# Loads by pairs of head groups, one solve load per chunk, five stores issued by ScalarE, and a refitted planner in a chunked RWKV and two-layer MLP kernel

## The chip, the cores and the metric

The kernel runs on one core of one Trainium2 chip. The metric is the device time of one execution in microseconds. Three runs of the kernel before gave 1331.51 us as their median (1323.21 to 1335.31).

## The reference

The first part is a recurrence over 768 steps for 4 batches x 8 heads with head size 40. Its output, laid out as 3072 tokens x 320, goes through two MLPs with 2048 hidden units.

```python
for t in range(S):
    y[:, :, t] = np.einsum('bhd,bhde->bhe', rt, state)
    Sa = np.einsum('bhde,bhe->bhd', state, at)
    state_decay = state * wt[:, :, None, :] - np.einsum('bhd,bhe->bhde', Sa, bt)
    state = state_decay + np.einsum('bhd,bhe->bhde', vt, kt)
...
h = np.maximum(x @ w_in, 0.0); x = h * h @ w_out
...
h = x @ w_in; g = np.where(h > 0.0, h, np.exp(np.minimum(h, 0.0)) - 1.0); out = g @ w_out
```

## The kernel before

The sequence is cut into 12 chunks of 64 steps. The 32 pairs of batch and head are worked on in 4 units of 8 (`hs(u)`). Within a chunk the recurrence becomes matrix products, and only the state is passed on from chunk to chunk. The MLPs work on the 256 tokens of a chunk.

For each chunk c, the steps that matter here are these, by function name.

- `scan`, `prep_a`, `prep_r`, `kb_rows`: running products of the decay, a and r scaled and split into three bf16 parts; the results go to the scratch tensors p_scr, a_scr, ya_scr and r_scr in device memory.
- `gram(c, u)` (line 954): loads ag from a_scr and gy from ya_scr (three loads, by `load_stacks`, line 883), multiplies gx with gy into PSUM (gram), masks one half into ag with VectorE, and copies the other half into bs with ScalarE. SP then stores bs to b_scr. bs has one buffer, so the copy of the next unit needs the store before it to have landed.
- `block_load(c, u)` (991) loads the 16 x 16 diagonal blocks of unit u from b_scr into the tile w, which the trace calls tt (free in chunk 1). `block_rest` (995) loads the other parts into lz (pb) and tb. `block_step` (1004) is the triangular solve: 15 steps of two VectorE instructions on w, which need all four units. `block_store` (1011) sends the result through n_scr and t_scr and loads it back as n1 (nt) and tb. `block_join` joins the blocks with small matmuls (join).
- `load_dyn(c, u)` (1065) loads vu, rf, rq (three loads by `load_stacks`) and w0 of one unit. The `dyn_*` functions are the part that depends on the state: f, u, bu, s (the new state), gh (which reads rq) and y. y goes to x_scr in device memory.
- `mlp1(c)` (782) loads x from x_scr, rounds it into xhi and xlo (`split_x`, 664) and runs the first MLP: h in PSUM (two buffers), its eviction by ScalarE, then accA and accB. `mlp2(c)` runs the second MLP.

The weights of both MLPs are loaded and converted in 24 pieces each (cs, ct; wl is TensorE's part of it). In two early chunks some tiles of odd units lie in weight tiles that are not yet filled (free); their PSUM tiles are called early.

The order of the instructions isn't the order of the code. The class `Order` records every operation of the main part, gives it a key (a due time from the tables OFF, SHIFT and BIAS plus 16 per chunk), and plays a list schedule: each engine takes, of the operations that are ready, the one with the lowest score. The costs in `cost` and constants such as ISSUE and SLOW say how long the planner takes an operation to be; `run` keeps a model of the clock and of the DMA rings. `emit` (522) writes the operations in the planned order, each engine's queue in that order, so all these instructions have one line in the profile (L527). Each engine executes its queue strictly in that order, SP's DMA issues too.

```python
AG, GX, BS, RAW, PL, VU, RV, W0, GH = 7, 1, 1, 2, 1, 2, 2, 2, 1
...
i = getattr(getattr(self.nc, name), op)(*a, **k)
```

Of the kernel before, what the change touches and what calls it, by code (L numbers as in the profile page):

```python
# [11 lines left out]
F32 = mybir.dt.float32  # L12
# [12 lines left out]
C = 64  # L25
NC = S // C
U = 4
HU = NH // U
# [21 lines left out]
T_W2, T_CL = 171, 197.1  # L50
OFF = {
# [9 lines left out]
}  # L61
SHIFT = {
    "prep": [-154.4, -2.921, -6.123, -4.768, -1.157, -0.04128, -7.933, -4.66, -8.011, -6.105, -9.653, -10.29],
    "gram": [-112.7, -7.051, -7.963, -1.157, -4.153, -5.312, -11.74, -10.6, -7.853, -6.692, -7.601, -13],
    "solve": [-21.31, -3.896, -6.557, 1.652, 0.3282, -6.306, -2.684, 6.628, 2.2, -4.088, -3.429, -14.15],
    "dyn": [-0.7973, -1.841, -2.488, 4.568, 0.9962, -2.788, -5.72, 5.713, 1.11, -2.128, -3.253, -3.913],
    "mlp": [-8.911, -10.83, -8.953, -8.113, -4.064, -4.485, -6.448, -8.254, -8.7, 3.455, 28.13, 32.75],
    "w": [-0.5978, -82.63, -108.8, -425.3, 353, 9.79, -83.32, 559.7, 134.3, 158.3, 376.1, -44.56],
    "mlp2": [24.41, 162.4, 191.8, 295.3, 373.5, 419.9, 490.2, 518.4, 570.3, 669.1, 674.1, 675.8],
}  # L70
BIAS = {
    "scan": [13.45, 2.846, 10.1, 3.45, -1.11, -3.105, 1.682, 21.9, 0, -2.434, 0.791, -0.6537],
# [125 lines left out]
class Order:  # L198
# [41 lines left out]
    def add(self, name, op, a, k):  # L240
# [13 lines left out]
        for aps, write in ((ins, False), (outs, True)):  # L254
            for x in aps:
# [10 lines left out]
                for e in h:  # L266
                    p, w, l2, h2 = e
                    hit = all(x1 <= y2 and x2 <= y1 for x1, y1, x2, y2 in zip(lo, hi, l2, h2))
                    if hit and (write or w) and p is not o:
                        o.deps.add(p)  # L270
# [1183 lines left out]
```

## Time and profile before

| what | value |
|---|---|
| median of three runs | 1331.51 us |
| the profiled execution | 1333.78 us |
| its span (first to last instruction) | 1331.9 us |
| mean granted TensorE clock | 0.925 |
| TensorE matmul busy (PE) | 1216.2 us, 91% |
| TensorE weight load busy (PEld) | 1113.1 us, 84% |
| VectorE busy (DVE) | 765.2 us, 57% |
| ScalarE busy (ACT) | 797.3 us, 60% |
| GpSimd busy (POOL) | 505.8 us, 38% |
| DMA | 158.01 MB, 119 GB/s in the mean |

The profile is of one execution on one core. A row of the timeline gives the start in us from the span's start, the duration, the engine, the operation with its output and inputs, and in brackets the idle time just before it with what ended it. A granted clock of 1.00 is full speed. SPq is SP's queue, which issues DMAs; the duration of such a row is that of the issue, not of the transfer. All names are the program's tile names without their buffer numbers.

### The profile page before, as it was taken

To read this page: it belongs to the slowest core of one execution; us is meant where nothing else is said; L and a number is where in the kernel's file an instruction comes from. 1 tells how busy PE (TensorE), PEld (TensorE's weight loads), DVE (VectorE), ACT (ScalarE), POOL (GpSimd) and SP (SyncE) were. 2 spreads that over 40 slices of the span, in tenths; PEclk is the share of its full clock that TensorE was granted. 3 is DMA by queue.
4 is the path that set the end of the run, shared out by engine and by line. 5 is a ranking of instruction groups with operands and counts; after the bars stand their busy time and mean duration, and the time that the engine had idled before them with its cause. 6 is when DMAs were issued, how large, how long until landed. Compare 5 with 4: busy or idle time off the path is not lost. (4 is left out here: it accounts for less than half of the span.)

```text
span 1331.9 us, 41778 instructions
## 1 busy us (share of the span) xinstructions
PE 1216.2 (91%) x17409; PEld 1113.1 (84%) x17409; DVE 765.2 (57%) x1434; ACT 797.3 (60%) x1536; POOL 505.8 (38%) x485
## 2 busy tenths in 40 slices
PE   2567879999999999999999999999999999999996
PEld 1446658789888988889888999999999999999996
DVE  6487766836743758666557634568844434434432
ACT  4576476647454657375576345555666666666663
POOL 2252131334441355243343222467733333333332
PEclk8667678979986999899999999999999999999998
DMA  8887885666565585655565423343300000000000
GB/s 269 227 226 173 225 214 149 168 158 166 135 171 128 156 211 142 164 119 151 133 179 146 93 61 108 101 142 115 94 21 21 21 21 21 21 21 21 21 16 17
DMA packets 244947, 158.01 MB, mean 119 GB/s; under 512 B 165648, under 2 KB 214160, under 8 KB 244752
## 3 DMA queue, kind: packets, MB, share of 16 engines
q1 hardware_dynamic: 244752, 155.27, 44.3%
q8 instruction: 139, 2.28, 0.7%
q14 instruction: 56, 0.46, 0.1%
HBM read 114.52 MB, written 40.69 MB: 117 GB/s over the span
## 5 line engine op out<-in xcount | busy, mean ns | idle before, releaser
L527 PE MATMUL h<-xhi,w 128*128 128x256 f32 x1920 | 513.6, 298 | 6.7 <-DVE r L527 6.0
L527 POOL TENSOR_TENSOR glo<-r,ghi 128x512 fp32r<-128x512 f32 x192 | 255.7, 1334 | 446.4 <-ACT ghi L527 208.6
L527 PEld LDWEIGHTS h<-xhi,w 128*128 128x128 f32 x1920 | 358.7, 192 | 24.6 <-DVE r L527 14.9
L527 PE MATMUL h<-xlo,w 128*128 128x256 f32 x1152 | 325.2, 285 | 0.0
L527 PEld LDWEIGHTS h<-xlo,w 128*128 128x128 f32 x1152 | 221.3, 192 | 0.3 <-POOL xlo L527 0.2
L527 ACT ACTIVATE r<-h 128x512 f32<-128x512 f32 x192 | 114.5, 596 | 134.7 <-PE h L527 123.1
L527 DVE SCALAR_TENSOR_TENSOR r<-e,r 128x512 f32<-128x512 f32 x96 | 75.6, 787 | 197.5 <-ACT r L527 197.4
L527 DVE TENSOR_TENSOR r<-h,r 128x512 f32<-128x512 f32 x192 | 132.2, 689 | 88.9 <-ACT ghi L527 76.8
L527 PE MATMUL accA<-w,ghi 128*128 128x320 f32 x768 | 179.4, 315 | 2.4 <-ACT ghi L527 2.3
L527 PE MATMUL accB<-w,ghi 128*128 128x320 f32 x768 | 178.4, 314 | 0.4 <-DVE o L527 0.4
L527 PEld LDWEIGHTS accA<-w,ghi 128*128 128x128 f32 x768 | 125.1, 191 | 4.2 <-ACT ghi L527 3.3
L527 PEld LDWEIGHTS accB<-w,ghi 128*128 128x128 f32 x768 | 125.4, 191 | 1.3 <-DVE o L527 0.6
L527 PE MATMUL accA<-w,glo 128*128 128x320 f32 x384 | 123.4, 321 | 1.3 <-POOL glo L527 0.7
L527 PE MATMUL accB<-w,glo 128*128 128x320 f32 x384 | 123.8, 322 | 0.0
L527 ACT CAST ghi<-r 128x512 fp32r<-128x512 f32 x96 | 59.1, 616 | 46.9 <-PE accB L527 23.5
L527 DVE SCALAR_TENSOR_TENSOR tt<-tt 128x1 f32<-128x1 f32 (+4 forms) x165 | 72.9, 442 | 24.6 <-DMA tt<-b_scr 20.0
L527 ACT ACTIVATE ghi<-r 128x512 fp32r<-128x512 f32 x96 | 60.4, 631 | 32.3 <-PE accB L527 31.4
L527 PEld LDWEIGHTS accA<-w,glo 128*128 128x128 f32 x384 | 73.3, 191 | 2.9 <-POOL glo L527 1.4
L527 PEld LDWEIGHTS accB<-w,glo 128*128 128x128 f32 x384 | 73.4, 191 | 1.4
L527 POOL TENSOR_TENSOR raw<-raw,pl 128x640 f32<-128x640 f32 x23 | 34.0, 1477 | 83.9 <-ACT pl L527 45.5
L527 PEld LDWEIGHTS <-gx 120*128 120x128 bf16 x1152 | 44.9, 108 | 25.0 <-issue 14.4
L527 POOL TENSOR_TENSOR kd<-kbt,ks 128x320 f32<-128x320 f32 x42 | 36.4, 866 | 77.1 <-ACT ks L527 77.1
(157 smaller groups left out, 2201.3 us busy)
## 6 DMA issues: line engine op xcount, KB each, us to landing
gy<-ya_scr SPq DMA_DIRECT2D x144, 120.0 KB
rq<-r_scr SPq DMA_DIRECT2D x144, 120.0 KB
cs<-w SPq DMA_DIRECT2D x32, 512.0 KB
kbt<-kbt SPq DMA_DIRECT2D x12, 640.0 KB
cs<-w SPq DMA_DIRECT2D x16, 384.0 KB
b_scr<-bs SPq DMA_DIRECT2D x48, 128.0 KB
ya_scr<-pl SPq DMA_DIRECT2D x12, 480.0 KB
r_scr<-pl SPq DMA_DIRECT2D x12, 480.0 KB
```

Of the source, the lines that this page charges most:

```text
L527: i = getattr(getattr(self.nc, name), op)(*a, **k)
```

## The change

Five edits, and one that follows from them.

- rq is one tile for a pair of units (`pair(u)`, 16 heads), filled by three loads when the even unit is loaded. There is one such buffer (RV // 2) where there were two single ones.
- ag is one tile for a pair, its lower part filled by one load. There are three such buffers where there were seven single ones.
- The diagonal blocks of all four units come in one load of 128 partitions (`block_load(c)`, due at what was the fourth unit's place) instead of four of 32.
- The four stores of bs to b_scr and the store to n_scr are issued by ScalarE (`nc.scalar.dma_start`), the rest of the DMAs by SP as before.
- The planner charges a DMA to the engine that issues it, takes 350 where it took 410 for an issue (plus 110 where one follows close on another on SP), has other constants for the clock, and orders VectorE and ScalarE where both touch one PSUM tile.
- All due times and biases are new numbers.

The matmuls, the operations of VectorE, ScalarE and GpSimd and their shapes are the same in number; SP has 192 DMA issues fewer and ScalarE 60 more.

```diff
-T_W2, T_CL = 171, 197.1
+T_W2, T_CL = 176.1, 213.4
-SWITCH, THIN, CHILL, BUSY = 0.1452, 5.835, 749.1, 0.5074
-YIELD = {"PE": (977.1, 24.8, 40.11), "DVE": (0.1731, 13.95, 2.022e+09), "ACT": (0.3328, 0.739, 1.114e+06), "POOL": (0.129, 32.88, 2.894e+05), "SP": (17.1, 0.6629, 215)}
-HOLD = {"PE": (2.65, 686.8), "DVE": (0.02736, 2.751e+04), "ACT": (0.2812, 674), "POOL": (1.353, 1.238), "SP": (0, 7.007)}
-ISSUE, STORE, LOAD, GUARD, COOL, WARM = 410.0, 2100.0, 2100.0, 600.0, 0.37, 0.6
-SLOW = {"b_scr": 300.0, "t_scr": 310.0, "tb": 160.0, "cs": 80.0, "vu": 200.0, "vs": 150.0, "wx": 80.0, "raw": 100.0, "n_scr": 250.0, "out": 100.0, "nt": 150.0, "rf": 50.0, "x": 100.0, "tt": 50.0, "k_scr": 100.0}
+SWITCH, THIN, CHILL, BUSY = 0.09435, 7.919, 28.43, 0.6976
+YIELD = {"PE": (2.587e+06, 6.959, 80.92), "DVE": (0.1309, 2.937, 5.164e+09), "ACT": (0.2351, 0.03413, 686.2), "POOL": (0.0002282, 4.888, 2.397e+06), "SP": (136.9, 4.725, 220)}
+HOLD = {"PE": (1.841, 924.1), "DVE": (0.7854, 9.898e+05), "ACT": (0.01352, 234.3), "POOL": (1.027e-05, 29.14), "SP": (0, 0.01961)}
+CLOSE = 110.0
+ISSUE, STORE, LOAD, GUARD, COOL, WARM = 350.0, 2100.0, 2100.0, 600.0, 0.40, 0.77
+SLOW = {"b_scr": 300.0, "t_scr": 310.0, "tb": 150.0, "cs": 60.0, "vu": 170.0, "vs": 170.0, "wx": 90.0, "raw": 90.0, "n_scr": 150.0, "out": 160.0, "nt": 100.0, "x": 40.0, "k_scr": 90.0, "a_scr": 80.0, "p_scr": 80.0}
...
-    "scan": -27.24, "pa": -24.91, "pr": -9.754, "kb": -27.22, "pl0": -19.04, "gr0": -17.12, "bl0": -9.569, "pl1": -19.19, "gr1": -17.24, "bl1": -13.25, "pl2": -18.08, "gr2": -14.83,
+    "scan": -27.03, "pa": -24.12, "pr": -14.35, "kb": -26.05, "pl0": -21.09, "gr0": -19, "pl1": -19.93, "gr1": -18.75, "pl2": -16.7, "gr2": -16.04, "pl3": -16.37, "gr3": -12.38,
...
-        self.clock, self.window, self.area, self.mode = 1.0, 0.0, 0.0, None
+        self.clock, self.window, self.area, self.mode = 0.5, 0.0, 0.0, None
-        self.tail = {"DVE": 0.0, "ACT": 0.0}
+        self.tail = {"DVE": 0.0, "ACT": 0.0, "SP": 0.0}
...
-                    if hit and (write or w) and p is not o:
+                    if (hit and (write or w) or t.space == PSUM and o.eng != p.eng and "PE" not in (o.eng, p.eng)) and p is not o:
...
-        if name == "sync":
+        if op == "dma_start":
...
-            o.area += stream * rep / 2.4 * min(1, rows / 128) * min(1, cols / 128)
+            o.area += stream * rep / 2.4 * max(r, 64) * max(c, 64) / 16384
...
-        if p.eng == "SP":
+        if p.dma is not None:
...
-            o.wait = o.eng in self.tail and any(p.eng != o.eng for p in o.deps)
+            o.wait = o.eng in ("DVE", "ACT") and any(p.eng != o.eng for p in o.deps)
...
-            o.late = max(o.late, p.end + (HOLD["SP"][1] if p.eng == "SP" else 0.0))
+            o.late = max(o.late, p.end + (HOLD["SP"][1] if p.dma is not None else 0.0))
...
-        elif o.eng == "SP":
-            self.free["SP"] = at + d
+        elif o.dma is not None:
+            if o.eng == "SP" and at - self.tail["SP"] < 150:
+                d += CLOSE
+            self.free[o.eng] = self.tail[o.eng] = at + d
...
-            if o.eng in self.tail:
+            if o.eng != "POOL":
...
 
+        def pair(u):
+            return slice(u * HU, (u + 2) * HU)
+
         def halves(u):
...
 
-        def load_stacks(dst, scr, u):
-            src = scr[:, hs(u)].rearrange("e n q t -> e (n q t)")
+        def load_stacks(dst, scr, heads):
+            src = scr[:, heads].rearrange("e n q t -> e (n q t)")
             for q in range(3):
...
         def gram(c, u):
-            ag = p1.tile([104, HU, C], F32, tag="ag", bufs=AG, name="ag")
+            if u % 2 == 0:
+                ex[c, u // 2, "ags"] = p1.tile([104, 2 * HU, C], F32, tag="ag", bufs=AG // 2, name="ag")
+                nc.sync.dma_start(out=ex[c, u // 2, "ags"][64:104], in_=a_scr[c][:, pair(u)])
+            ag = ex[c, u // 2, "ags"][:, hs(u % 2)]
             ex[c, u, "ag"] = ag
-            nc.sync.dma_start(out=ag[64:104], in_=a_scr[c][:, hs(u)])
             early = c < EP and u % 2
             gy = (mlp if early else p0).tile([120, HU, 3, C], BF16, tag="xhi" if early else "gy", bufs=XB if early else GX, name="gy")
-            load_stacks(gy, ya_scr[c], u)
+            load_stacks(gy, ya_scr[c], hs(u))
             gx = (mlp if early else p0).tile([120, HU, 2 * C], BF16, tag="r" if early else "gx", bufs=2 if early else GX, name="gx")
...
             nc.scalar.copy(out=flat(bs)[b], in_=flat(ps)[b])
-            nc.sync.dma_start(out=ap(b_scr[c][:], u * HU * HB, [[C, C], [HB, HU], [1, C]]), in_=bs[b])
+            nc.scalar.dma_start(out=ap(b_scr[c][:], u * HU * HB, [[C, C], [HB, HU], [1, C]]), in_=bs[b])
 
...
 
-        def block_load(c, u):
-            nc.sync.dma_start(
-                out=ex[c, "w"][32 * u:32 * u + 32, 0], in_=ap(b_scr[c][:], u * HU * HB, [[HB // 4, 32], [C, 16], [1, 16]]))
+        def block_load(c):
+            nc.sync.dma_start(out=ex[c, "w"][:, 0], in_=ap(b_scr[c][:], 0, [[HB // 4, 128], [C, 16], [1, 16]]))
 
...
             nc.scalar.copy(out=w[:, 0], in_=w[:, 1].rearrange("p r t -> p t r"))
-            nc.sync.dma_start(out=n_scr[c].rearrange("n h t r -> (n h) t r"), in_=w[::2, 0])
+            nc.scalar.dma_start(out=n_scr[c].rearrange("n h t r -> (n h) t r"), in_=w[::2, 0])
             for q in range(2):
...
             nc.sync.dma_start(out=rf, in_=io["rt"][c][:, hs(u)])
-            rq = p1.tile([120, HU, 3, C], BF16, tag="rq", bufs=RV, name="rq")
-            ex[c, u, "rq"] = rq
-            load_stacks(rq, r_scr[c], u)
+            if u % 2 == 0:
+                ex[c, u // 2, "rqs"] = p1.tile([120, 2 * HU, 3, C], BF16, tag="rq", bufs=RV // 2, name="rq")
+                load_stacks(ex[c, u // 2, "rqs"], r_scr[c], pair(u))
+            ex[c, u, "rq"] = ex[c, u // 2, "rqs"][:, hs(u % 2)]
             w0 = p1.tile([D, HU, C + 1], F32, tag="w0", bufs=W0, name="w0")
...
                 at("gram", f"gr{u}", c, lambda u=u: gram(c, u))
-                at("gram", f"bl{u}", c, lambda u=u: block_load(c, u))
+            at("gram", "bl3", c, lambda: block_load(c))
 
         def solve(c):
             at("gram", "bn", c, lambda: blocks(c))

```

SP's queue around the solve of chunk 0, before: b_scr_111 is chunk 0's scratch, ag and a_scr_76 belong to chunk 1, cs are weight pieces.

```order
L527 DMA b_scr_111<-bs 64x8x64
L527 DMA tb<-b_scr_111 32x8x32
L527 DMA ag<-a_scr_76 40x512 x4
L527 DMA tt<-b_scr_111 32x16x16
L527 DMA tb<-b_scr_111 32x8x32
L527 DMA b_scr_111<-bs 64x8x64
L527 DMA ya_scr_88<-pl 128x5x384
L527 DMA raw<-ax 128x640
L527 DMA cs<-w 128x1024 x2
L527 DMA tt<-b_scr_111 32x16x16
L527 DMA pb<-b_scr_111 16x32x16 x2
```

The same place on SP after the change.

```order
L528 DMA tb<-b_scr_111 32x8x32
L528 DMA ag<-a_scr_76 40x1024 x2
L528 DMA tb<-b_scr_111 32x8x32
L528 DMA cs<-w 128x768
L528 DMA ya_scr_88<-pl 128x5x384
L528 DMA tt<-b_scr_111 128x16x16
L528 DMA pb<-b_scr_111 16x32x16 x2
```

The stores are gone from SP, the loads tt are one, and one weight piece of 384 KB stands ahead of it where two of 512 KB stood.

ScalarE's queue from the third copy of bs to the fourth, chunk 0, before.

```order
L527 COPY bs<-gram 64x512
L527 ACTIVATE cs<-cs 128x512
L527 CAST pl<-raw 128x10x64
L527 ACTIVATE cs<-cs 128x384
L527 CAST w_182<-cs 128x512
L527 COPY bs<-gram 64x512
```

And after the change.

```order
L528 COPY bs<-gram 64x512
L528 DMA b_scr_111<-bs 64x8x64
L528 CAST pl<-raw 128x10x64
L528 COPY bs<-gram 64x512
L528 DMA b_scr_111<-bs 64x8x64
L528 CAST w_179<-wl 128x2x64
```

Each copy is followed by its own store, and the weight conversions stand behind the last of them.

TensorE's queue at the first matmul of the MLP (h), before. nt and pb are chunk 2's, y, gh and kbt chunk 1's.

```order
L527 MATMUL fa<-vs,ag 64x40 x16
L527 MATMUL str<-ident,vs 40x40 x8
L527 MATMUL y<-gh,kbt 40x64 x8
L527 MATMUL join<-nt,pb 32x16 x32
L527 MATMUL h<-xhi,w_178 128x256
L527 MATMUL h<-xlo,w_178 128x256
```

And after the change, where the y from rf is unit 0 of chunk 1, the first y that reads the state.

```order
L528 MATMUL wl<-cs,ident 128x128
L528 MATMUL wl<-w_446,minus 128x128
L528 MATMUL h<-xhi,w_178 128x256
L528 MATMUL h<-xlo,w_178 128x256
L528 MATMUL y<-rf,ss_193 40x64 x8
L528 MATMUL y<-gh,kbt 40x64 x8
```

The first h has moved ahead of that y and so ahead of the rest of chunk 1's state-dependent part and of chunk 2's join.

## Rows read from the trace of the kernel before

**Rows 1.** Stretch, busy us (PE, PEld, DVE, ACT, POOL), granted clock, DMA share, GB/s.
```profile
0.00:176.00 176.00, 110.47 (x1799) 85.64 (x1801) 121.28 (x251) 104.76 (x208) 50.82 (x58) 0.71 0.81 223
176.00:205.00 29.00, 20.62 (x345) 15.67 (x346) 17.88 (x30) 20.41 (x43) 11.67 (x14) 0.76 0.82 219
205.00:450.00 245.00, 232.11 (x4376) 207.24 (x4376) 148.98 (x328) 138.40 (x276) 83.42 (x82) 0.87 0.61 155
450.00:900.00 450.00, 435.72 (x7790) 398.04 (x7789) 273.12 (x536) 262.11 (x524) 185.23 (x181) 0.99 0.52 134
```

**Rows 2.** Timeline of TensorE, 172 to 208 us: start, us, engine, operation.
```profile
175.95 0.64 PE L527 MATMUL y<-rf,ss 40*40 40x64 f32 x16
...
197.48 1.46 PE L527 MATMUL gram<-gy,gx 120*128 120x64 bf16 x24 [3.06 <-ACT gx L527]
...
204.77 0.38 PE L527 MATMUL h<-xhi,w 128*128 128x256 f32 x1
```

**Rows 3.** Instructions on the tile x, 100 to 230 us: min/median/max ns, starts.
```profile
L527 SPq DMA_DIRECT2D x<-x_scr x4: 431/512/587, 170.6 to 188.3; - x4
L527 ACT CAST xhi<-x x3: 404/407/408, 181.0 to 190.7; 128x256 fp32r<-128x256 f32 x3
```

**Rows 4.** Waits of SP's queue, 47 to 57 us: us, times, longest.
```profile
SPq L527 <- DMA b_scr<-bs: 2.1, 1, 2.1
```

**Rows 5.** Timeline of all engines, 45.5 to 57 us.
```profile
45.74 0.59 SPq L527 DMA_DIRECT2D b_scr<-bs  x1
...
50.94 0.32 SPq L527 DMA_DIRECT2D tt<-b_scr  x1
...
52.24 0.58 ACT L527 COPY bs<-gram 64x512 f32<-64x512 f32 x1
...
52.84 0.58 SPq L527 DMA_DIRECT2D b_scr<-bs  x1
...
56.56 0.38 SPq L527 DMA_DIRECT2D tt<-b_scr  x1
```

**Rows 6.** Timeline of VectorE, 47 to 90 us.
```profile
47.39 1.60 DVE L527 TENSOR_SCALAR ct<-cs 128x512 uint32<-128x512 uint32 x1
...
52.42 0.56 DVE L527 SCALAR_TENSOR_TENSOR cs<-cs 128x384 uint32<-128x384 uint32 x1
...
64.41 0.16 DVE L527 SCALAR_TENSOR_TENSOR tt<-tt 128x1 f32<-128x1 f32 x1 [3.35 <-DMA tt<-b_scr]
...
89.48 0.39 DVE L527 TENSOR_REDUCE tt<-tt 128x15 f32<-128x225 f32 x1
```

**Rows 7.** DMA issues by tile, whole span: min/median/max ns of an issue.
```profile
L527 SPq DMA_DIRECT2D ag<-a_scr x48: 272/320/1187, 22.9 to 718.4; - x48
...
L527 SPq DMA_DIRECT2D rq<-r_scr x144: 272/331/3315, 37.2 to 841.9; - x144
...
L527 SPq DMA_DIRECT2D tt<-b_scr x44: 307/399/1336, 40.1 to 744.3; - x44
...
L527 SPq DMA_DIRECT2D b_scr<-bs x48: 581/602/1552, 34.6 to 736.0; - x48
...
L527 SPq DMA_DIRECT2D n_scr<-tt x11: 480/492/621, 91.0 to 762.4; - x11
```

**Rows 8.** Four stretches with a lower clock, columns as in rows 1.
```profile
275.00:300.00 25.00, 22.35 (x399) 19.37 (x399) 6.69 (x17) 9.42 (x21) 6.59 (x7) 0.65 0.65 169
300.00:325.00 25.00, 24.57 (x445) 22.84 (x444) 16.32 (x42) 19.54 (x39) 12.77 (x13) 0.94 0.54 145
375.00:400.00 25.00, 22.22 (x482) 20.36 (x482) 11.26 (x24) 13.85 (x31) 9.03 (x13) 0.77 0.62 142
400.00:425.00 25.00, 25.00 (x331) 22.48 (x327) 8.02 (x13) 11.80 (x23) 3.02 (x3) 0.55 0.45 115
```

**Rows 9.** TensorE's waits, 205 to 900 us: the longest for ScalarE.
```profile
PE stk L527 <- ACT bs L527: 1.9, 3, 1.4
```

**Rows 10.** Waits of SP's queue, whole span.
```profile
SPq L527 <- PE gh L527: 25.9, 18, 4.4
```

More of the change, by code (lines that the diff above doesn't have):

```diff
@@ L49 @@
 WPE = True
-T_W2, T_CL = 171, 197.1
+T_W2, T_CL = 176.1, 213.4
 OFF = {
[9 rows of a table removed]
[9 rows of a table added]
 }
 SHIFT = {
[L63 to L69, printed above, removed]
+    "prep": [-252.4, -24.58, -12.17, -10.47, -1.272, -5.026, -6.748, -9.319, -3.061, -9.193, -7.383, -4.819],
+    "gram": [-202, -7.468, -15.62, -13.63, -3.948, -6.708, -10.78, -9.453, -7.021, -13.38, -5.386, -8.988],
+    "solve": [-28.55, -6.792, -6.956, 2.77, 2.25, 3.314, 4.85, 8.249, 5.394, -1.603, -2.223, -3.919],
+    "dyn": [-7.115, -0.164, 3.141, 2.877, -0.4202, 0.4353, 1.525, 8.763, 6.207, 2.873, -0.4381, 2.331],
+    "mlp": [-10.63, -6.306, -5.107, -5.92, 1.545, -0.1849, -0.4791, -1.937, -0.9688, 15.42, 23.84, 67.31],
+    "w": [0.7824, 28.74, 9.338, -281.5, 595.9, 206.1, 37.91, 698.2, 70.89, 213.2, 242.8, -75.76],
+    "mlp2": [58.68, 193.7, 207.6, 396.4, 457.9, 483.3, 553.6, 587.1, 624.8, 641, 672.7, 697.4],
@@ L70 @@
 }
 BIAS = {
-    "scan": [13.45, 2.846, 10.1, 3.45, -1.11, -3.105, 1.682, 21.9, 0, -2.434, 0.791, -0.6537],
[109 rows of a table removed]
-    "out": [-123.3, -123.5, 27.59, 54.12, 26.52, 14.75, -1.5, 25.13, 21.71, -99, 33.7, -1.649],
-    "rg": [-114.5, -18.01, 41.33, 0, 3.137, -75.9, 25.32, 14.95, -49.15, -93.66, 7.806, -9.546],
-}
-SWITCH, THIN, CHILL, BUSY = 0.1452, 5.835, 749.1, 0.5074
-YIELD = {"PE": (977.1, 24.8, 40.11), "DVE": (0.1731, 13.95, 2.022e+09), "ACT": (0.3328, 0.739, 1.114e+06), "POOL": (0.129, 32.88, 2.894e+05), "SP": (17.1, 0.6629, 215)}
@@ L187 @@
-HOLD = {"PE": (2.65, 686.8), "DVE": (0.02736, 2.751e+04), "ACT": (0.2812, 674), "POOL": (1.353, 1.238), "SP": (0, 7.007)}
-ISSUE, STORE, LOAD, GUARD, COOL, WARM = 410.0, 2100.0, 2100.0, 600.0, 0.37, 0.6
-SLOW = {"b_scr": 300.0, "t_scr": 310.0, "tb": 160.0, "cs": 80.0, "vu": 200.0, "vs": 150.0, "wx": 80.0, "raw": 100.0, "n_scr": 250.0, "out": 100.0, "nt": 150.0, "rf": 50.0, "x": 100.0, "tt": 50.0, "k_scr": 100.0}
+    "scan": [13.26, 6.176, -5.325, 0, -2.635, -5.793, 1.988, 28.93, 1.106, -1.397, -12.63, 8.316],
[107 rows of a table added]
@@ new lines @@
+    "out": [1.344, -2.018, 20.81, -1.778, 3.498, 62.02, 32.87, 20.64, 20.19, -2.632, 7.53, 18.95],
+    "rg": [-22.09, -29.07, -24.26, -86.91, -107.9, -26.03, -44.44, -5.98, -21.02, -164.5, -37.79, -30.08],
+}
+SWITCH, THIN, CHILL, BUSY = 0.09435, 7.919, 28.43, 0.6976
+YIELD = {"PE": (2.587e+06, 6.959, 80.92), "DVE": (0.1309, 2.937, 5.164e+09), "ACT": (0.2351, 0.03413, 686.2), "POOL": (0.0002282, 4.888, 2.397e+06), "SP": (136.9, 4.725, 220)}
+HOLD = {"PE": (1.841, 924.1), "DVE": (0.7854, 9.898e+05), "ACT": (0.01352, 234.3), "POOL": (1.027e-05, 29.14), "SP": (0, 0.01961)}
```

232 rows, old and new, of tables (BIAS, OFF) are left out of this document.

## The prediction

> **What bounds the kernel now.** I read the busy time by stretches first. From 450 to 900 us TensorE works 435.7 of 450 us at a granted clock of 0.99 [rows 1]. There is nothing to win there, and nothing behind it, where only matmuls of the second layer are left. From 205 to 450 us it is busy 232.1 of 245 us, so 12.9 us are idle, but the clock is 0.87. From 0 to 176 us it is busy 110.5 of 176, at 0.71. From 176 to 205 it is busy 20.6 of 29, at 0.76. So what can be gained lies ahead of 450 us: 65.5 us idle, then 8.4 us, then 12.9 us, and the time that a lower clock costs. The lower clock is one of two levels, 1.2 against 2.4 GHz, so a stretch of length L with mean clock c loses at most L x (1 - c) of full-speed work.
>
> Next I looked at how the end of the startup is set. The first matmul of the MLP (h) starts at 204.77 us; from there on TensorE has independent work in hand. The first y from rf, which is unit 0 of chunk 1, runs at 175.95 us [rows 2]. The rounding of chunk 0's x, the input of h, was done three times between 181.0 and 190.7 us, and its loads were issued from 170.6 to 188.3 [rows 3]. So h could have had input some 20 us before it ran; the order held it back. Between 176 and 205 us TensorE meanwhile sat in front of gram for 3.06 us at one place, waiting for ScalarE's gx [rows 2].
>
> Last, the path that feeds chunk 0. Its four stores of bs to b_scr end with one at 45.74 and one at 52.84 us on SP's queue. Between them SP stood 2.1 us for a landing of b_scr [rows 4], at the load tt<-b_scr of 50.94, which reads what the store of 45.74 wrote [rows 5]. The last such load went out at 56.56 and the first step of the solve ran at 64.41, after VectorE had waited 3.35 us for it; the last step ended at 89.87 [rows 5, 6].
>
> **The change, part by part.** The program's counts are what the change says: per chunk 2 ag issues fewer, 6 rq, 3 tt, and 4 b_scr and 1 n_scr stores go from SP to ScalarE. By the medians [rows 7] SP loses over 12 chunks 24 x 0.32 + 72 x 0.33 + 36 x 0.40 + 48 x 0.60 + 12 x 0.49 = 81 us of issue. That is no time by itself: SP is on the path only where a load for which an engine waits stands behind others. Ahead of the last x load of chunk 0 the two orders have 238 and 184 issues, but 41.6 and 40.6 MB (the latter with the stores that ScalarE issues). So the queue gets shorter and the bytes do not.
>
> (A) The MLP starts earlier in TensorE's order. In the new order the first h stands directly ahead of the first y from rf. In the trace of before that place is 176 us. The input was rounded from 181 us on, so the stretch from about 181 to 205 us gets MLP work where it has gaps now. It can give back the 8.4 us of idle time and at most 29 x 0.24 = 7.0 us of clock, 15.4 together. It can also give less than nothing, if h in front of the attention's pieces delays chunk 2 and the same gaps return later: -5. Some gaps will stay, since attention still waits for ScalarE. I take 6 of the 8.4 and 3 of the 7.0, that is 9 us.
>
> (B) The solve of chunk 0 starts earlier. bs has one buffer, so the fourth copy needs the third store to have landed, which it had by 50.94 at the latest. That copy ended just ahead of the store at 52.84. In the new order ScalarE has one row between those two copies, besides the store, where it had four. If the landing takes as long as before, some 1.3 us are won (50.94 against a copy start 0.6 us ahead of 52.84). If the store starts with the copy and doesn't queue behind SP's loads, the two stores come closer than 7.1 us and more is won. VectorE also has less ahead of the first step: the conversions of two weight pieces stood there from 47.39 to 52.98 us [rows 6], now one smaller piece does. Against it stands the single load, four times the elements at once: the last quarter alone took 56.56 to 64.41, with everything queued ahead of it, so at the worst 3 us more. Bounds -3 and +10. I take 4, near the lower rows, because the first half of the chain (grams, their loads) is not touched. What is late next is the join, which waits for nt<-n_scr as now.
>
> The Trainium skill ("DMA: Bandwidth & Descriptors", section "Issuing engines are not separate DMA queues") says that transfers run on the same 16 DMA engines whichever engine issues them, and that a second issuer saves issue time alone. Row and rule meet in the DMA share, 0.81 and 0.82 up to 205 us [rows 1]. By the rule (B) would be 1.3 us instead of 4, and the sum 14 instead of 17.
>
> (C) Clock and gaps after 205 us. At 275 to 300 us the clock is 0.65 with 2.65 us idle: 8.75 + 2.65 = 11.4 us lost. At 300 to 325, 375 to 400 and 400 to 425 us 1.5, 5.75 and 11.25 us go to the clock [rows 8]. In the last of these TensorE was busy throughout: there it was the order (many small 32-row matmuls), not a wait. In the first it fell after a stretch with gaps. Fewer issues ahead of a load make such gaps smaller. No row tells what the new order does to the clock, so I bound it: from all 27.25 us of clock in these four rows to two new spells like that of 400 us, -22. I take 5, half of the one spell that has gaps ahead of it, rounded down.
>
> (D) ScalarE pays for 60 issues. The trace shows none of its own; the nearest rows are SP's for the same stores, 0.60 and 0.49 us: 48 x 0.60 + 12 x 0.49 = 35 us, longest 1.55 us each [rows 7]. ScalarE is busy 138.4 of 245 and 262.1 of 450 us [rows 1], so most of it falls into its gaps. Behind a store on ScalarE stand the evictions of h, gx and vu, for which TensorE waits. Such waits are few now: from 205 to 900 us the longest row is 1.9 us in all, for bs [rows 9]. 35 us more on 400 busy is 9% more load, and 9% of waits of this size is well under 1 us. Bounds 0 and 35. I take 1, near that row.
>
> The rq buffer: two single tiles become one pair, so a pair's load waits for both gh of the pair before it. SP waits for gh now 18 times, 25.9 us in total [rows 10]. If that doubles, SP still has 81 us fewer issues. gh feeds y and the MLP's x, which have a chunk of slack, not the state. I cost it at nothing, at worst 5 us; once x arrives late that cover is gone and TensorE waits at h.
>
> **Sum.** 9 + 4 + 5 - 1 = 17 us. The profiled execution took 1333.8 us for a span of 1331.9, which is 2.3 us over the median of 1331.5. 1333.8 - 17 = 1316.8; from the median it would be 1314.5. I take 1316.
>
> **The rivals.** *More of the same mechanism.* If (A) gives 15, (B) 8 and the whole spell at 275 us goes (11), less 1: 33 us, 1301. For it: the gaps are there in the rows. Against it: attention's own waits (on ScalarE, on VectorE) are not removed by a shorter SP queue.
>
> *The DMA engines are the bound of the startup, not SP.* For it: a DMA share of 0.81 over the first 176 us, and bytes ahead of x that fall by 1 MB of 41.6 only. Then x arrives when it did, (B) is 1, (A) is worth half, (C) nothing: 1333.8 - 5 - 1 + 1 = 1329. This is also what the cited rule would make of it. Against it: SP itself stood still for a landing inside the chain of chunk 0, for 2.1 us.
>
> *ScalarE becomes the bound (the other side).* Each h needs a ScalarE eviction, and h has two PSUM buffers. [...] If TensorE waits out the whole 35 us: 1333.8 - 17 + 35 = 1352; I set 1350. It decides from the point where TensorE's waits on ScalarE from 205 to 900 us exceed some 20 us. Against it: ScalarE is idle more than 40% there.
>
> *The new order brings more low clock.* Two more spells like that of 400 to 425 us, and no (C): 1333.8 - 13 + 1 + 22 = 1344.
>
> **How the numbers follow.** A difference of under 1% (13.3 us, so above 1318 and below 1345) is about what a measurement of this kernel cannot tell from none. Forecast 0.48, with a spread of its own from 1307 to 1325: 0.30 of it faster, 0.18 within 1%. More of the same 0.16, all faster. DMA-bound 0.18: 0.17 within, 0.01 slower. ScalarE 0.12 slower, low clock 0.06 slower. That makes 0.46, 0.35 and 0.19. The range takes in the 1301 case with its bounds (the full 15.4, 10 and 17.5 would be 1291) and reaches up to short of the ScalarE case: 1292 to 1343.
>
> **What would show it.** (A): first h near 180 us, and fewer than 65 us idle ahead of it. (B): first solve step at 60 to 61 us, last bs store of chunk 0 near 49. (C): a clock above 0.87 from 205 to 450 us. (D): ScalarE's issues near 0.6 us each, and TensorE's waits for ScalarE after 205 us within 2 us of now. It is wrong if h starts at 195 us or later, if the clock from 205 to 450 us falls below 0.85, or if the waits on ScalarE pass 20 us.

## The result and the profile after

The changed kernel took 1316.47 us (median of 18 runs, 1304.09 to 1327.28) against 1336.02 us (18 runs) of the kernel before, measured beside it: a ratio of 0.985, 95% interval 0.9822 to 0.9878. A second measurement of the same two kernels gave 0.9854 (0.9815 to 0.9892). That is 1.5% faster, some 20 us, where the forecast was 1316 us. The profiled execution took 1321.71 us for a span of 1319.9, so it is one of the slower ones, 12.0 us of span under that of before. The profile of the second measurement (called the later profile) has a span of 1311.7 us. Where a reading hangs on the difference I give both. The ratios leave out a kernel's slow runs, and as that takes 7 of 12 from the kernel with the filled stretch below, its median over all runs is given too.

Busy time by stretches of the changed kernel, first profile, columns as in [rows 1]: PE busy (count), PEld, DVE, ACT, POOL, granted clock, DMA share, GB/s.

```profile
0.00:176.00 176.00, 105.15 (x1710) 81.06 (x1712) 115.58 (x241) 100.48 (x203) 54.87 (x58) 0.86 0.79 218
176.00:205.00 29.00, 24.19 (x354) 19.79 (x352) 18.56 (x35) 21.96 (x45) 11.50 (x13) 0.71 0.79 206
205.00:450.00 245.00, 230.82 (x4363) 206.80 (x4360) 159.18 (x335) 144.17 (x289) 97.84 (x94) 0.88 0.63 161
450.00:900.00 450.00, 441.53 (x8000) 405.84 (x7998) 276.49 (x548) 266.25 (x533) 184.74 (x179) 1.00 0.54 137
```

Against [rows 1]: the idle time of 176 to 205 us fell from 8.4 to 4.8 us, as the sum wanted. Ahead of 176 us it rose from 65.5 to 70.8, so up to 205 us TensorE is idle 75.7 us where it was 73.9. In the later profile it is idle 74.6 us up to 176 and 79.7 up to 205 us. The startup gained nothing. From 450 to 900 us, where I had seen "nothing to win", idle time fell from 14.3 to 8.5 us.

The stretches of [rows 8] in the changed kernel, and 550 to 600 us behind them:

```profile
275.00:300.00 25.00, 23.70 (x563) 21.51 (x564) 14.78 (x29) 12.94 (x27) 15.36 (x14) 0.90 0.69 173
300.00:325.00 25.00, 25.00 (x390) 22.89 (x387) 14.38 (x36) 14.46 (x30) 7.67 (x7) 0.69 0.52 149
375.00:400.00 25.00, 24.79 (x403) 22.46 (x398) 21.74 (x43) 19.27 (x37) 16.49 (x16) 1.00 0.61 177
400.00:425.00 25.00, 22.10 (x538) 20.57 (x538) 15.64 (x30) 10.85 (x20) 8.41 (x8) 0.93 0.80 179
...
550.00:600.00 50.00, 48.69 (x971) 44.27 (x965) 32.68 (x72) 32.23 (x68) 26.30 (x25) 1.00 0.65 162
```

The low clock of 275 to 300 us (0.65 before) and of 375 to 425 us (0.77 and 0.55) is mostly gone. A new one stands at 300 to 325 us (0.69, where 0.94 was). In the later profile the four clocks are 1.00, 0.86, 0.93 and 0.81. Of 550 to 600 us the kernel before has this row:

```profile
550.00:600.00 50.00, 44.94 (x854) 40.41 (x855) 30.19 (x66) 27.59 (x58) 19.58 (x21) 0.90 0.55 140
```

For the account I use one measure for a stretch of length L: idle time plus L x (1 - clock), the upper bound of what the lower clock costs. The clock is read to two decimals, which leaves up to 2.3 us open in 450 us. These rows give the measure, with those of 450 to 900 us in [rows 1] and above: first the kernel before, then the changed kernel's first profile, then its later one.

```profile
205.00:300.00 95.00, 87.63 (x1702) 76.07 (x1702) 61.75 (x126) 54.99 (x112) 28.99 (x29) 0.87 0.61 155
300.00:450.00 150.00, 144.48 (x2675) 131.18 (x2675) 87.23 (x202) 83.41 (x165) 54.43 (x53) 0.86 0.61 155
```

```profile
205.00:300.00 95.00, 89.73 (x1825) 78.17 (x1823) 60.36 (x128) 57.30 (x116) 31.82 (x32) 0.90 0.62 155
300.00:450.00 150.00, 141.09 (x2546) 128.63 (x2543) 98.82 (x208) 86.87 (x173) 66.02 (x62) 0.87 0.64 164
```

```profile
205.00:300.00 95.00, 91.40 (x1930) 79.56 (x1930) 62.77 (x138) 59.55 (x121) 33.35 (x32) 0.95 0.67 171
300.00:450.00 150.00, 139.93 (x2608) 127.66 (x2610) 99.86 (x204) 89.97 (x179) 64.06 (x62) 0.90 0.62 159
450.00:900.00 450.00, 439.65 (x7812) 403.81 (x7809) 281.63 (x544) 262.72 (x525) 189.60 (x183) 1.00 0.53 137
```

| lost, us | 205 to 300 | 300 to 450 | 450 to 900 | sum | span |
|---|---|---|---|---|---|
| before | 7.4 + 12.4 | 5.5 + 21.0 | 14.3 + 4.5 | 65.1 | 1331.9 |
| after, first profile | 5.3 + 9.5 | 8.9 + 19.5 | 8.5 + 0 | 51.7 | 1319.9 |
| after, later profile | 3.6 + 4.8 | 10.1 + 15.0 | 10.4 + 0 | 43.9 | 1311.7 |

The sums differ from before by 13.4 and 21.2 us, the spans by 12.0 and 20.2. So the whole gain lies behind 205 us, in stretches 205 to 300 and 450 to 900, and most of it is lower clock that is no longer there (37.9 us before, 29.0 and 19.8 after). The part from 205 to 300 us is that of 275 to 300: idle time and clock there were 11.4 us and are 3.8 and 0.9.

The start of the MLP, the solve of chunk 0 and the rounding of chunk 1's x, in the timelines of TensorE, VectorE and ScalarE, all engines mixed:

```profile
47.79 0.58 ACT L528 COPY bs<-gram 64x512 f32<-64x512 f32 x1 [3.79 <-DMA b_scr<-bs]
48.40 0.59 ACTq L528 DMA_DIRECT2D b_scr<-bs  x1
...
52.89 0.58 ACT L528 COPY bs<-gram 64x512 f32<-64x512 f32 x1 [2.51 <-DMA b_scr<-bs]
53.50 0.59 ACTq L528 DMA_DIRECT2D b_scr<-bs  x1
57.97 0.37 SPq L528 DMA_DIRECT2D tt<-b_scr  x1
...
60.72 1.75 DVE L528 SCALAR_TENSOR_TENSOR cs<-cs 128x384 uint32<-128x384 uint32 x1
62.39 0.14 DVE L528 SCALAR_TENSOR_TENSOR tt<-tt 128x1 f32<-128x1 f32 x1
...
184.21 0.34 PE L528 MATMUL h<-xhi,w 128*128 128x256 f32 x1
...
290.69 0.40 ACT L528 CAST xhi<-x 128x256 fp32r<-128x256 f32 x1
```

h starts at 184.21 us (204.77 in [rows 2]). The solve starts at 62.39 us (64.41 in [rows 6]; 63.14 in the later profile), behind a conversion of VectorE and not behind its load. The last store of bs goes out at 53.50 us, later than the 52.84 of [rows 5]; ScalarE now stands in front of the copy for the landing of the store before it. The row at 290.69 is the last rounding of chunk 1's x. In the kernel before it is this one:

```profile
305.57 0.40 ACT L527 CAST xhi<-x 128x256 fp32r<-128x256 f32 x1
```

DMA issues of the changed kernel (answering to [rows 7]) and TensorE's longest waits from 205 to 900 us (answering to [rows 9]):

```profile
L528 ACTq DMA_DIRECT2D b_scr<-bs x48: 582/594/652, 33.6 to 737.4; - x48
...
L528 ACTq DMA_DIRECT2D n_scr<-tt x11: 495/500/1526, 89.6 to 769.1; - x11
```

```profile
PE join L528 <- issue: 7.8, 4, 5.7
PE gram L528 <- DMA gy<-ya_scr: 2.2, 3, 0.9
PE rpt L528 <- DVE kbt L528: 2.0, 4, 1.0
PE s L528 <- DVE gh L528: 1.7, 1, 1.7
PE fa L528 <- ACT f L528: 1.7, 2, 1.5
PE gh L528 <- DMA rq<-r_scr: 1.5, 1, 1.5
```

A store costs ScalarE 0.594 us, as estimated. The longest row of TensorE waiting for ScalarE is 1.7 us here and 2.3 us in the later profile:

```profile
PE stk L528 <- ACT bs L528: 2.3, 1, 2.3
```

All such rows together are 8.4 us in the kernel before, 3.3 and 5.9 us in the changed one.

### The profile page after: what moved, and what is told of

It reads as the page before. It is cut to its first block, busy times and chain, and to the rows that moved or that the text cites. A ratio compares the mean times of both kernels' runs of the same rounds, so it can differ in the third digit from the quotient of the medians.

```text
span 1319.9 us, 41548 instructions
## 1 busy us (share of the span) xinstructions
PE 1207.2 (91%) x17409; PEld 1105.7 (84%) x17409; DVE 769.4 (58%) x1434; ACT 792.5 (60%) x1536; POOL 510.3 (39%) x485
## 5 line engine op out<-in xcount | busy, mean ns | idle before, releaser
L528 DVE SCALAR_TENSOR_TENSOR r<-e,r 128x512 f32<-128x512 f32 x96 | 81.3, 847 | 182.0 <-ACT r L528 180.9
L528 DVE SCALAR_TENSOR_TENSOR tt<-tt 128x1 f32<-128x1 f32 (+4 forms) x165 | 71.4, 433 | 15.9 <-DMA tt<-b_scr 8.5
L528 ACT ACTIVATE r<-r 128x512 f32<-128x512 f32 x96 | 60.7, 632 | 2.0
L528 ACT COPY gx<-stk 120x1024 bf16<-120x1024 bf16 x48 | 48.5, 1011 | 22.1 <-PE stk L528 13.0
```

## The experiments

First question: do the loads, the stores or the numbers (the planner's constants and its due times) carry the gain? Theory 1, formed from the first profile: the new order fills the thin stretch at 385 to 425 us. R1: SP's relief. R2: the earlier start of the MLP. Edits to `emit` leave the planned order as it is and change one thing in it.

**Stores back on SP (changed kernel).**

```diff
             for name, op, a, k in o.calls:
+                if op == "dma_start":
+                    name = "sync"
```

> The changed kernel in its own planned order, but its 60 stores to b_scr and n_scr are issued by SP at their planned places. Theory 1 (the gain is the new order of the MLP among the small matmuls around 385 to 425 us, the issue relief itself is worth little): within 3 us of the changed kernel, so 0.983 to 0.988 of the kernel before. Rival R1 (relief of SP's queue and ScalarE's issues are the gain): at least 8 us are lost, 0.991 or more, and first solve step of chunk 0 at 64 us or later instead of 62.4.

Measured: 1320.62 us, ratio 0.9883 (0.9829 to 0.9937). The value lies between the two expectations, and the interval holds 0.985 and 0.991. But the first solve step came at 61.59 us, earlier than with ScalarE's stores, which R1 does not allow.

**Stores on ScalarE (kernel before).**

```diff
             for name, op, a, k in o.calls:
+                if op == "dma_start" and k["out"].tensor.name[:5] in ("b_scr", "n_scr"):
+                    name = "scalar"
```

> The kernel before in its own planned order, but the 48 stores to b_scr and 12 to n_scr are issued by ScalarE at their planned places. Theory 1: 0.998 to 1.002 of the kernel before; the low clock at 400 to 425 us stays (0.55). Rival R1: 0.993 or less. The other side (ScalarE pays for each issue): 1.005 or more.

Measured: 1332.16 us, 0.9949 (0.9912 to 0.9986). The stores alone give a little, between the two theories, and cost nothing. The clock of 400 to 425 us stayed low (0.65). The first solve step came at 63.46 us, 0.95 us earlier, where the prediction had 1.3 for a landing that SP no longer waits out ahead of a store. That is no shown difference: in the pulled and the filled kernel below, which are the kernel before up to there, it came at 63.11 and 66.34 us.

**Pair loads issued as halves (changed kernel).**

```diff
+                    if n[:2] in ("rq", "ag"):
+                        m = w.shape[1] // 2
+                        parts = [dict(out=w[:, s], in_=x[:, s]) for s in (slice(0, m), slice(m, 2 * m))]
+                    elif n[:2] == "tt" and "b_scr" in x.tensor.name:
+                        parts = [dict(out=w[q:q + 32], in_=x[q:q + 32]) for q in (0, 32, 64, 96)]
```

> The changed kernel in its own planned order, but each pair load of rq and ag is issued as two halves and each load tt<-b_scr as four of 32 partitions, one behind the other at the place of the single one: 132 issues more on SP, some 47 us by their medians, the same bytes and buffers. If SP's issues are a part of the gain: 4 us or more are lost, 0.988 to 0.993. If only the order and the stores on ScalarE count: 0.983 to 0.987.

Measured: 1316.22 us, 0.9843 (0.9791 to 0.9894). 132 more issues on SP cost nothing that can be seen. The uncertainty against 0.9854 is some 9 us and could hide the 4 us of the expectation; the next kernel, with every issue of before and the whole gain, shows that fewer issues are not needed for it.

**The numbers without the structure, and the structure without the numbers.** The first has the changed planner and tables on the single loads, the seven and two single buffers, four solve loads and SP's stores of before (bl0 to bl2 get offsets of -11.45, -14.76 and -13.27 and no bias). The second has the changed loads, buffers and stores, with the tables, constants and clock model of before.

```diff
-            nc.scalar.dma_start(out=ap(b_scr[c][:], u * HU * HB, [[C, C], [HB, HU], [1, C]]), in_=bs[b])
+            nc.sync.dma_start(out=ap(b_scr[c][:], u * HU * HB, [[C, C], [HB, HU], [1, C]]), in_=bs[b])
...
-            at("gram", "bl3", c, lambda: block_load(c))
+                at("gram", f"bl{u}", c, lambda u=u: block_load(c, u))
```

```diff
-T_W2, T_CL = 176.1, 213.4
+T_W2, T_CL = 171, 197.1
...
-ISSUE, STORE, LOAD, GUARD, COOL, WARM = 350.0, 2100.0, 2100.0, 600.0, 0.40, 0.77
+ISSUE, STORE, LOAD, GUARD, COOL, WARM = 410.0, 2100.0, 2100.0, 600.0, 0.37, 0.6
```

> The changed kernel's planner and numbers, the structure of before: single loads and buffers of rq and ag, four loads of the solve's input per chunk, all stores on SP. If the gains add up (earlier start of the MLP about 9 us, stores and loads about 10): 0.990 to 0.996, first h before 190 us. If the numbers only fit their own structure: 1.000 or more.

> The changed kernel's loads, buffers and stores on ScalarE with the planner and numbers of before. If the gains add up: 0.990 to 0.996, first h near 200 us. If the numbers have to fit the structure: 1.000 or more.

Measured: the numbers alone 1318.84 us, 0.9851 (0.9806 to 0.9897); the structure alone 1346.7 us, 1.0076 (1.0046 to 1.0106). This is the clearest pair of the study. The numbers give the whole gain on the old structure (the planner's constants and the due times were not tried apart). The structure under the old numbers is slower than before. They don't add up, and both expectations of a half gain are missed. With the numbers alone the first h ran as late as this, and the gain was there all the same:

```profile
213.68 0.36 PE L530 MATMUL h<-xhi,w 128*128 128x256 f32 x1
```

Its gain lies in part elsewhere than the changed kernel's:

```profile
205.00:300.00 95.00, 87.18 (x1596) 75.68 (x1596) 67.68 (x151) 59.98 (x121) 28.35 (x28) 0.95 0.63 162
300.00:450.00 150.00, 139.24 (x2573) 127.59 (x2573) 94.93 (x191) 89.18 (x176) 65.99 (x63) 0.91 0.64 160
450.00:900.00 450.00, 434.97 (x7838) 398.73 (x7834) 271.69 (x537) 258.85 (x516) 184.45 (x176) 0.99 0.51 135
```

By the measure above it loses 12.6, 24.3 and 19.5 us, where the kernel before loses 19.8, 26.5 and 18.8. Its span is 1321.9 us. So 205 to 300 us gains here as well, and 450 to 900 us does not.

So neither SP's relief nor an early h is needed. Second question: what in the order is it?

**The thin stretch of before filled, that of after thinned.** Both move TensorE's MLP matmuls only later, by a table of knots, and what hangs on them with them.

```diff
+            t = o.start
+            if o.eng == "PE" and o.label and o.label[0] == "mlp":
+                t = max(t, np.interp(t, *KNOTS))
+            t = max([t] + [p.end + late[p] for p in o.deps if late.get(p)])
+            late[o] = t - o.start
...
-        for o in sorted(made, key=lambda o: (o.start, o.seq)):
+        for o in sorted(made, key=lambda o: (o.start + late[o], o.seq)):
```

The knots, in ns of the planner's time (from, to), for the kernel before and for the changed kernel:

```diff
+KNOTS = [0, 305500, 325200, 339900, 369600, 5000000], [0, 305500, 326900, 348300, 369600, 5000000]
```

```diff
+KNOTS = [0, 353000, 368000, 398000, 5000000], [0, 353000, 383000, 398000, 5000000]
```

> The kernel before, its order kept, but TensorE's matmuls of the MLP between 305 and 370 us of the planner's time (about 345 to 429 us of the profile) are spread evenly by moving some of them up to 8 us later, so that the stretch with few of them is shorter. Theory 1: the clock of 400 to 425 us rises from 0.55 to over 0.8 and the time falls by 5 to 10 us, 0.992 to 0.996. Rivals R1 and R2 (the earlier start of the MLP is the gain): nothing to win there, 0.999 to 1.004.

> The changed kernel, but the MLP's matmuls planned from 353 to 398 us (about 389 to 447 us of the profile) come at half the density first and at twice the density afterwards, as a thin stretch like that of the kernel before at 385 to 425 us. If the filled stretch is the gain (theory 1, which the spread of before's stretch has not borne out): clock of 400 to 425 us below 0.75 and 0.991 to 0.995. If the low clock there is paid in any order: 0.983 to 0.988.

Measured, filled: 0.9954 (0.9899 to 1.001), with a median of 1340.12 us over all runs against 1336.23. The clock rose nearly as far as was wanted, but no gain can be told from it:

```profile
400.00:425.00 25.00, 24.15 (x440) 21.33 (x427) 10.42 (x19) 15.09 (x30) 4.55 (x6) 0.80 0.64 170
```

Measured, thinned: 1324.46 us, 0.9882 (0.9847 to 0.9917). Its clock there was 0.98, so the thinning made no low clock at all and the expectation is missed. Against 0.9854 it lost 0.3%, with an uncertainty of 0.5. Neither run decides on theory 1: the first value lies in its range with 1 in the interval, and the second made no stretch of that kind. What speaks against it is the table: from 300 to 450 us as a whole the kernel before loses 26.5 us and the changed kernel 28.4 and 25.1, so what the one stretch won was paid beside it.

**The first h held back (changed kernel).** The same edit with other knots.

```diff
+KNOTS = [0, 167000, 167200, 204600, 5000000], [0, 167000, 187000, 204600, 5000000]
```

> The changed kernel with the first h matmuls (from 167 us of the planner's time) held back to 187 us, where the kernel before has them, so the first h runs at about 204 us instead of 184. Theory 1: 0.984 to 0.988, since the earlier start was given back ahead of 205 us. Rival R2 (the earlier start is the gain, 9 us as the prediction had it): 0.991 or more.

Measured: 1323.91 us, 0.9932 (0.9895 to 0.9969), h at 202.52 us. Against 0.9854 this is some 10 us lost, with an uncertainty of 7 (the two half intervals, 0.0037 and 0.0038, in quadrature are 0.0053). In its profile TensorE does 21.06 us of work from 176 to 205 us instead of 24.19; the span of that execution, 1319.0 us, doesn't show the loss. The 10 us can be what an early h is worth, as term (A) had it, or what it costs to move any piece of a fitted order; the run doesn't part the two. The numbers alone show an order that does as well without an early h.

**The MLP moved as a whole, both ways.** Theory 2: the MLP's matmuls stand earlier and denser from 205 to 300 us. In the kernel before, they and the MLP's evictions and loads are pulled forward as far as inputs allow (first edit). In the changed kernel TensorE's part is held back (second, the edit above with other knots).

```diff
+KNOTS = [180000, 283000, 325000, 400000, 420000, 5000000], [165000, 265000, 310000, 398000, 420000, 5000000]
...
+            if o.label and o.label[0] == "mlp" and t > KNOTS[0][0]:
+                t = min(t, np.interp(t, *KNOTS))
+            new[o] = max([t] + [new[p] + p.end - p.start + 60 for p in o.deps if p in new and (t < o.start or new[p] > p.start)])
```

```diff
+KNOTS = [0, 167000, 167200, 259500, 330000, 392000, 5000000], [0, 167000, 187000, 275000, 336000, 392000, 5000000]
```

> The kernel before with the order of the attention kept and the first MLP of chunks 0 to 2 moved forward among it, as far as its inputs allow and by up to 16 us of the planner's time (chunk 0's first h by 6, chunk 1 by 15, fading to nothing at 420 us). Theory 2 (the gain is that the MLP's matmuls come earlier and denser among the attention's from 205 to 300 us, so that the input of chunk 1 can be rounded 15 us earlier): xhi of chunk 1 ready near 290 us instead of 305, and 0.986 to 0.993. Rival (the MLP only trades places with the attention, which pays the same back): 0.998 to 1.005.

> The changed kernel with TensorE's first-MLP matmuls held back: chunk 0 starts 20 us later, as in the kernel before, and ends 15 us later, chunk 1 follows, all back in place at 392 us of the planner's time. Theory 2: xhi of chunk 1 ready near 305 us, and 0.990 to 0.996, at least 5 us lost. Rival (only a trade of places): 0.983 to 0.987.

> The changed kernel once more, unedited, on the same chip and against the same runs of the kernel before as the three kernels beside it: 0.982 to 0.988.

Measured: pulled 1351.69 us, 1.0141 (1.0103 to 1.0179); held 1348.58 us, 1.0122 (1.0084 to 1.0159); the changed kernel beside them 0.9854. Both directions lose, 19 us from the kernel before and 36 us from the changed one. By the knots no piece was moved by more than 18 us in the first and 20 in the second. The pulled kernel:

```profile
205.00:300.00 95.00, 87.65 (x1670) 76.47 (x1664) 57.50 (x122) 52.59 (x107) 30.34 (x30) 0.91 0.55 145
300.00:450.00 150.00, 135.71 (x2655) 120.67 (x2653) 89.94 (x193) 84.02 (x169) 52.34 (x53) 0.87 0.61 156
450.00:900.00 450.00, 438.25 (x7774) 399.77 (x7769) 261.73 (x534) 254.25 (x506) 173.68 (x171) 0.95 0.50 129
```

It rounds chunk 1's x at 294.42 us, 11 us earlier, and loses 15.9 us up to 300 us by the measure above, where before loses 19.8. Then it pays: 33.8 against 26.5, and 34.3 against 18.8. The held kernel loses at once. It rounds chunk 1's x at 313.85 us, later than the 305 that was wanted. Its profile is of its fastest execution (1337.87 us against the median of 1348.58), so not all of the loss is in these rows:

```profile
205.00:300.00 95.00, 82.68 (x1712) 72.27 (x1709) 56.38 (x118) 51.23 (x102) 24.48 (x25) 0.90 0.56 145
300.00:450.00 150.00, 132.99 (x2457) 119.20 (x2454) 93.82 (x186) 80.47 (x161) 63.76 (x60) 0.95 0.60 156
```

TensorE is idle 12.3 and 17.0 us there, where the changed kernel has 3.6 to 5.3 and 8.9 to 10.1. No single wait explains it; its longest rows from 205 to 450 us are small and of many kinds:

```profile
PE y L535 <- DVE gh L535: 3.6, 3, 2.0
PE stk L535 <- DVE sp L535: 3.6, 3, 2.1
PE stk L535 <- ACT bs L535: 2.8, 2, 1.5
```

My reading, which no run shows, is that a held MLP matmul no longer covers the wait of the attention's piece behind it. Theory 2 in its simple form falls: earlier is not better by itself. So does its rival, since a mere trade of places would have cost nothing.

**Three buffers of x (changed kernel).**

```diff
-            x = mlp.tile([128, TOK], F32, tag="x", bufs=2, name="x")
+            x = mlp.tile([128, TOK], F32, tag="x", bufs=3, name="x")
```

> The changed kernel with three buffers of the MLP's input x where it has two, so that a chunk's third load needn't wait for the rounding of the first; the planner then makes another order from the same numbers. If the change of chunk (the old x is read until its last h, then round, load, round) thins TensorE's work by some 4 us each time up to 600 us: 0.978 to 0.985. If the numbers only fit the plan they were made for: 0.987 or more.

Measured: 1342.79 us, 1.0076 (1.0047 to 1.0105). A constraint less, and 2.2% slower than the changed kernel. The likely reason is the one expected, that the planner makes another order from numbers that were fitted to this one; it was not tried apart. No version tried beats the changed kernel.

## Why the prediction was right in its sum and wrong in its terms

The forecast of 1316 us was met, and its sum of 17 us stands against 20. The terms don't stand: (A) and (B) were to give 13 us and gave nothing that shows, and (C) gave 8 to 16 us more than its 5. That the sum came out is luck.

- **(A), 9 us.** The mechanism came in part: h at 184 us, idle from 176 to 205 us down by 3.6 us (3.3 in the later profile). The step that failed is the one that counted only the stretch from 181 to 205 us. Ahead of 176 us the new order is idle 5.3 us longer (9.1 in the later profile), so up to 205 us nothing is left. The sign named for h, "fewer than 65 us idle ahead of it", is missed with 70.8 and 74.6. That holding h back costs some 10 us is no proof of the term, as said above.
- **(B), 4 us.** The first solve step came 2.0 us earlier (1.3 in the later profile), not 3.4 to 4.4, the last store of bs at 53.50 us instead of near 49. The step from ScalarE's own issues to stores that come closer was half right: 5.1 us between them instead of 7.1, because bs has one buffer and the landing is still waited for, on ScalarE (3.79 and 2.51 us) and on SP (its waits for b_scr are 59.2 us in 25 where they were 21.2 in 13). With the numbers alone the solve started at 60.77 us with SP's stores, so SP's relief was not what set it. The Trainium skill ("DMA: Bandwidth & Descriptors", section "Issuing engines are not separate DMA queues") had it that a second issuer saves issue time alone. Nothing in the runs speaks against it: the DMA share up to 176 us is 0.79 after 0.81, and the stores alone are worth 0.5%.
- **(C), 5 us.** This term was mis-sized and holds the gain: 13 to 21 us by the two profiles, within its bounds of -22 and 27. The reason given for it, fewer issues ahead of a load, is refuted by the numbers alone, which keep every issue, and the split loads agree. Of the 27.25 us of clock in the four rows that I priced, 12.0 and 10.0 are left. The spell at 275 to 300 us, half of which I took, went by 7.6 and 10.5 us with its gaps; what 375 to 425 us gave was paid elsewhere between 300 and 450 us. "There is nothing to win there", of 450 to 900 us, was wrong by 8 to 10 us by the measure above.
- **(D), -1 us, and rq at 0.** ScalarE's stores took 0.594 us, and TensorE's waits for ScalarE, 8.4 us in all before, were 3.3 and 5.9; the kernel before with these stores alone was not slower (0.9949). The rival of ScalarE as the bound never came near its 20 us. In the changed kernel gh waits 1.5 us for rq (2.5 in the later profile). The structure alone costs 0.8% under the old numbers. Which of its edits costs that was not tried apart, so rq at nothing is shown for the new order alone.

Two readings of the prediction were wrong beside the terms. The "many small 32-row matmuls" of 400 to 425 us are 96 of 331 matmuls there and take less time than 14 of one form of h, as the groups of that stretch in the kernel before show:

```profile
L527 PE MATMUL h<-xhi,w 128*128 128x256 f32 x14 | 6.6, 485 | 0.0
...
L527 PE MATMUL fa<-f,tb 32*32 32x40 f32 x64 | 2.6, 263 | 0.0
...
L527 PE MATMUL fa<-vu,tb 32*32 32x40 f32 x32 | 1.3, 264 | 0.0
```

And the range's lower end takes 17.5 us for (C), which no row gives; with (C)'s own bound of 27.25 it would be 1281.

Of the rivals, the one with the DMA engines as the bound came nearest for the startup (it gave (A) and (B) 6 us, where nothing was gained) and had the rest wrong, 1329 us; more of the same (1301) and more low clock (1344) did not come.

What stays open: which placements of the new order carry the 20 us. The gain is shown to come with the numbers, to lie behind 205 us, and to vanish when the changed kernel's MLP is held back. The clock of 275 to 300 us, 0.65 before, is 0.90 to 1.00 with the new numbers on either structure. But it is 1.00 in the pulled and the three-buffer kernels too, which are slower than the kernel before, so a full clock there is not enough. No single piece was found that has the gain alone.

## What to carry to other kernels

Where one engine runs its queue strictly in order and a planner fills its gaps, test the order and the structure apart before crediting either: here the order alone gave the whole gain, and the edits that a reader would have praised were not needed for it: the stores alone gave 0.5%, the whole structure under the old numbers cost 0.8%. A term that no row prices should get a bound and a share of the forecast to match, and a stretch called full is worth recounting as idle time plus clock. An order fitted to its kernel can be a sharp optimum: here moving the first MLP as a whole or adding one buffer cost 1.4 to 2.7%.

## What was not expected of the hardware

The same kernel's TensorE clock differs from one execution to the next: over six executions of the changed kernel on one chip, in the second measurement, its mean is 0.928 to 0.959. In the two profiles of the changed kernel it was 0.86 and 0.76 from 0 to 176 us, and 0.90 and 0.95 from 205 to 300 us. In the startup the lower clock cost nothing that shows: the later execution, whose row this is, began h at 181.37 us instead of 184.21 and had a span 8.2 us shorter.

```profile
0.00:176.00 176.00, 101.39 (x1744) 77.89 (x1744) 118.03 (x248) 102.17 (x208) 53.65 (x58) 0.76 0.80 223
```

So the product of length and clock up to 176 us says little of what can be won there, since TensorE is busy only 101 to 110 of these 176 us in the three profiles, and a single profile settles no difference under about 8 us, the distance of these two.
